# Attention and MLP in one kernel: a latest end for TensorE's side work in each step, and the first VectorE units one step sooner

## The chip, the core and the metric

The kernel runs on one core of a Trainium2 chip. The core has a matrix engine (TensorE, PE in the profile; its weight loads are listed as PEld), VectorE (DVE), ScalarE (ACT), GpSimd (POOL) and SyncE (SP), which here issues most of the DMAs. Each engine runs its own list of instructions in order, and the lists are tied together by semaphores. The metric is the device time of one execution in microseconds. It is given as the median of several runs.

## The reference

The kernel computes one block with an attention branch and an MLP branch on the same input, mixed by a gate for each token. Sizes: 2048 tokens, width 640, 32 heads of 20, MLP width 1536, bf16 inputs.

```python
def _A_ref(x, wqkv, wo):
    B, S, D = x.shape
    H = 32; Dh = D // H
    qkv = (x @ wqkv).reshape(B, S, 3, H, Dh).transpose(2, 0, 3, 1, 4)
    q, k, v = qkv[0], qkv[1], qkv[2]
    scores = jnp.einsum("bhqd,bhkd->bhqk", q, k) * Dh ** -0.5
    p = _softmax(scores, axis=-1)
    o = jnp.einsum("bhqk,bhkd->bhqd", p, v)
    return o.transpose(0, 2, 1, 3).reshape(B, S, D) @ wo

def _B_ref(x, w1, b1, w2):
    h = jnp.einsum("bsd,df->bsf", x, w1) + b1
    sp = jnp.log1p(jnp.exp(-jnp.abs(h))) + jnp.where(h > 0, h, 0)
    act = h * jnp.tanh(sp)
    return jnp.einsum("bsf,fd->bsd", act, w2)

g = _sigmoid((x * gate_w).sum(-1, keepdims=True))
return g * _A_ref(A_x, A_wqkv, A_wo) + (1 - g) * _B_ref(A_x, B_w1, B_b1, B_w2)
```

## The kernel before, in words

**Units and slots.** The attention is cut into units. A unit is one head (j, four heads to a group g), one tile of 128 keys (kt) and one chunk of 512 queries (c): a score matmul of 32 x 128 weights against 512 columns gives 128 x 512 scores in one PSUM bank. There are 32 heads x 16 tiles x 4 chunks = 2048 units. Three units make a slot, so there are 683 slots (the last has two units). The score banks are two sets of three banks. Slot s uses set s mod 2, so the scores of slot s can only be written once the exponential of slot s - 2 has read its set.

**The exponential of a slot.** ScalarE takes the exponentials of a whole slot in one ACTIVATE (line 1083): 128 x 1536, a *wide* one. In some slots the third unit is given to VectorE instead. ScalarE then takes only two units, 128 x 1024, a *narrow* one. VectorE works its unit out in four operations: it moves the scores out of PSUM with scale and bias (line 1111), and then runs three polynomial steps (lines 1127 and 1129) that build the exponential in the bits of an integer. The function `choose` decides whether a slot gives a unit away, by the planner's estimate of how much VectorE has left to do. Results of ScalarE go to a ring of five buffers (ETS).

**Products with v.** When the four heads of a key tile have their exponentials, TensorE multiplies them with v in one pass (four matmuls side by side, line 1197, function `emit_pv`), and sums up in the PSUM bank ACC over the 16 key tiles of a group. The units of VectorE get passes of their own (`emit_off`).

**Fillers.** All other matmuls are tasks that are worked off in pieces between the score blocks: the projections for q, k and v (lines 541, 607, 629, 705, 732), the Gram matrices for a safety bound (774), the MLP's two layers (851 and 910) and the output projection (934). Some are *forced*: when their due step has come they are issued at once, whatever the time. TensorE also gets passes without use (`spin`, line 1471, and repeated score blocks) where the planner finds it too thinly used.

**The planner.** The order is written by Python code before the program is built. A class `Plan` keeps an estimated time for each engine (`pl.now`) and adds every instruction's cost, with waits, as it is put in an engine's list. A loop goes over the steps. In step s it puts in: forced tasks that are due, the exponential of slot s, the choice for slot s + 2 and its score block, then up to two passes of products with v (`emit_pv(step, 2)`), then fillers as long as they end before `limit`, and then VectorE's work that fits. So on TensorE, what is put in after the score block of slot s + 2 in step s stands ahead of the score block of slot s + 3.

Costs that matter here, in us, as the planner has them: a wide exponential 1.335 (`EXP`), a narrow one 0.908 (`EXP_PAIR`), a pass of 512 columns 0.213 (`PASS`), a change of the kind of matmul 0.1 (`SWITCH`), a hop between engines 0.1 (`HOP`). Before the change the fillers' limit is the estimated end of the exponential of the step plus one wide exponential and a hop, whatever comes next; the products with v have no limit. `CALM` is the step from which `choose` is asked: slot `CALM` + 2 is the first that may give a unit away.

A second plan (`full`) stands in the program for inputs whose scores are too large for the fast exponential; a flag worked out on the chip chooses it, and with these inputs it does not run. Each engine loads that flag once (line 1399).

Of the kernel before, what the change touches and what calls it, by code (L numbers as in the profile page):

```python
# [47 lines left out]
SWITCH = 0.1  # L48
COL = 1 / 2400.0
PASS = CW * COL  # L50
EXP = 1.335
STREAM = 0.48
SPUN = 0.6
EXP_PAIR = 0.908
# [24 lines left out]
LAG = 9  # L79
SPARE = 3.5  # L80
WINDOW = 3.41
CALM = 4
PACKED = 10
PACKED_Q = 12
Q_AT = 100
# [3 lines left out]
H_AT = 150  # L89
H_STEP = 12.5  # L90
THIN = 0.09
OVER = 0.2
CUTS = ((0, 256), (256, 256))

# [124 lines left out]
def bass_gated_mix__softmax_full_mha__dense_activation_mish__prompt_kernel(  # L219
# [114 lines left out]
    NSLOT = -(-NC * NG * NKT * HG // SLOT)  # L334


    off = {}
    off_units = {}

    def attention(pl, fast):  # L340
# [84 lines left out]
        def flush(done):  # L425

            while not done():
                ready = [lane for lane in soon if lane]
                first = min(ready, key=lambda lane: (lane[0][2]().t1 if lane[0][2] else 0.0, lane[0][3]))
                first.popleft()[1]()  # L430
# [595 lines left out]
        started = {}  # L1026
        queue = deque()
        hold = {"until": 0}
        acc_free = [m_acc if fast else pl.add("dve", lambda e: e.memset(PS[:, ACC, :], 1.0))]

        def compose(s, extra=None):
# [19 lines left out]
        def score_mms(s, some, deps):  # L1051

            op = None
            for r in range(max(len(subs(*u[:3])) for u in some)):
                began = False
                for i, (c, g, kt, j) in enumerate(some):
                    if r >= len(subs(c, g, kt)):
                        continue
                    tile, cols, of_q = subs(c, g, kt)[r]
                    cost = max(extent(c, g)[1] * COL, THIN)  # L1060
                    op = pl.add("pe", lambda e, i=i, g=real(g), tile=tile, j=j, cols=cols, c=c, of_q=of_q: e.matmul(  # L1061
# [99 lines left out]
        def emit_off(group, last, force=False):  # L1161

            mine = off_units.get(group, []) if fast else []
            begun = started.get((group, "off"), 0)
            there = 0
            while there < len(mine) and mine[there] in unit_done and (
                    force or unit_done[mine[there]].t1 + HOP <= pl.now["pe"]):
                there += 1
            whole = there == len(mine)
            if there - begun > 1 or last and whole:  # L1170
                rows = []
                for u in mine[begun:there]:
                    if not rows or u[3] in [v[3] for v in rows[-1]]:
                        rows.append([])
                    rows[-1].append(u)
                for row in rows:
                    lasts = pv([(u, ei(off_home[u]).bitcast(BF16)[:, 0::2], [unit_done[u]]) for u in row])
                    for k, u in enumerate(row):
                        ei_free[off_home[u]] = lasts[k]
                started[(group, "off")] = there  # L1180
            return whole
# [21 lines left out]
        def emit_pv(step, passes):  # L1203

            while passes and step >= hold["until"]:
                if not queue:
                    return
                c, g, kt, _ = queue[0][2]
                emit_off((c, g), False)
                n = HG - sum(u[2] == kt for u in off_units.get((c, g), ()) if fast)  # L1210
                if len(queue) < n:
                    return
                if kt == tiles(c, g) - 1 and not emit_off((c, g), True):
                    if step < NSLOT - 1:
                        return
                    flush(lambda: emit_off((c, g), True, True))
                passes -= 1
                some = [queue.popleft() for _ in range(n)]
                lasts = pv([(u, ETS[:, s % NETS, i, :], [e_op[s]]) for s, i, u in some])
                for k, (s, i, u) in enumerate(some):  # L1220
                    op = pv_slot[s] = lasts[k]
                    pv_left[s] -= 1
                if kt == tiles(c, g) - 1:
                    hold["until"] = step + PV_HOLD
                    group_done(c, g, step, op)
# [264 lines left out]
        for step in range(NSLOT + 40):  # L1490
            now["step"] = step
            if step >= NSLOT and not queue and not tasks and not any(k >= step for k in at):
                break

            for t in [t for t in tasks if t.forced and t.due <= step]:
                while now["open"] not in (None, t):
                    put(now["open"])
                while t in tasks:
                    put(t)
            if step < NSLOT:  # L1500
                emit_e(step)
            if fast and area[0] and not w2_load and len(h_done) >= FIRST and all(ei_free[(0, b)] != "busy" for b in range(3)):
                load_w2()
            if acts and safe(acts[0][0]) < pl.now["act"] and mish_free():
                acts.popleft()[1]()
            ahead = able = 0.0
            rate = behind = 0.0
            lag = max((step - t.due for t in tasks if not t.forced and t.ready() is None), default=0)
            for t in tasks:
                slack = max(1, t.due - AHEAD * t.forced - step)  # L1510
                ahead += t.left()
                rate = max(rate, ahead / slack)
                if t.forced or t is now["open"] or t.ready() is not None:
                    able += t.left()
                    behind = max(behind, able / slack)
            now["rate"] = rate
            if step + 2 < NSLOT:
                compose(step + 2, choose(step + 2) if fast and step >= CALM and (step < slot_of(0, 1, 0) or behind < CATCH_UP and (lag < LAG or backlog() < SPARE) and room()) else None)
                emit_s(step + 2)
                to_come = pv_ready() * PASS  # L1520
                if owed + rate > 0.1 and pick(pl.now["pe"] + 0.8):
                    to_come += min(owed + rate, 0.4)
                fill_up(to_come, False)

                if fast and step + 2 in off:
                    emit_x(step + 2)
            limit = pl.now["act"] + EXP + HOP if step < NSLOT else 1e9
            owed = min(owed + rate, 1.0) if step < NSLOT else 1e9
            if fast and step < NSLOT and now["open"] and now["open"].left() <= min(owed + OVER, limit - pl.now["pe"] - PASS - SWITCH):
                t = now["open"]  # L1530
                while t in tasks:
                    put(t)
                    owed -= t.cost
            emit_pv(step, 2 if step < NSLOT - 1 else 99)

            while owed > 0:
                t = pick(limit)
                if t is None:
                    break
                put(t)  # L1540
                owed -= t.cost
            fill_up(0.0, True)
            for fn in at.pop(step, []):
                fn()
            work(pl.now["act"] + 0.5 if step < NSLOT else 1e9)
# [112 lines left out]
    fast = Plan("f_")  # L1658
# [55 lines left out]
```

## Time and profile before

| | |
|---|---|
| time, median of 3 runs | 866.54 us (866.3 to 866.74) |
| profiled execution: its own time | 866.43 us |
| profiled execution: span from the first to the last instruction | 864.6 us |
| granted TensorE clock, mean | 0.999 |
| busy: ScalarE, VectorE, TensorE | 847.8, 829.4, 756.3 us |

In the rows of the profile, times are microseconds unless marked ns. A row of a group reads: line, engine, operation, tile written <- tiles read, shapes, count | busy time, mean ns of one | idle time of the engine just before them, and what ended most of it. A row of the timeline reads: start, length, engine, line, operation, count, and in brackets the engine's idle time before it with what ended it; neighbouring instructions of the same line and tile are merged into one row, which bears the shapes of the first. The lengths of merged rows run from the first start to the last end. In the row of the granted clock each digit is a fortieth of the span, and 9 is 90% or more. A row of the chain of waits reads: start, length, what, count.

### The profile page before, as it was taken

The page shows a single profiled execution, that of the slowest core. Times are in us where ns is not written, and L with a number is a line of the kernel's source. Part 1 is how long each engine was busy: PE and PEld are TensorE (multiplying, and loading weights), DVE is VectorE, ACT ScalarE, POOL GpSimd, SP SyncE. Part 2 cuts the span into 40 slices and gives each one's busy share as a digit, 9 for nine tenths or more (in the row PEclk, how much of TensorE's full clock was granted, in tenths as well). Part 3 has the DMA queues.
Part 4 walks back from the last instruction along what each step waited for, and adds up shares of the span by engine and source line. Part 5 has one row for each costly group of instructions (what it writes and reads, how often), then busy time and mean ns, then how long its engine had stood idle before and what let it go on. Part 6 is the DMA issues. An engine that isn't in the chain of part 4 may idle for free.

```text
span 864.6 us, 15494 instructions
## 1 busy us (share of the span) xinstructions
PE 756.3 (87%) x6342; PEld 259.5 (30%) x6342; DVE 829.4 (96%) x1330; ACT 847.8 (98%) x714; POOL 7.3 (1%) x14
## 2 busy tenths in 40 slices
PE   8988998889889888898888888898888888899886
PEld 3333332223322332232223333333322333333232
DVE  4799999999999999999999999999999999999996
ACT  6999999999999999999999999999999999999996
POOL 2000000000000000000000000000000000000000
PEclk9999999999999999999999999999999999999999
DMA  9711310012233221401111211112112211000001
GB/s 215 95 61 36 107 46 19 16 60 69 78 93 89 67 62 53 123 26 38 44 39 44 71 34 58 44 36 60 55 44 60 59 51 41 28 25 29 18 14 35
DMA packets 76318, 48.42 MB, mean 56 GB/s; under 512 B 22104, under 2 KB 71888, under 8 KB 76192
## 3 DMA queue, kind: packets, MB, share of 16 engines
q1 hardware_dynamic: 73872, 46.86, 20.1%
q8 instruction: 52, 0.85, 0.4%
q10 hardware_dynamic: 2256, 0.47, 0.3%
q0 software_dynamic: 112, 0.01, 0.1%
q14 instruction: 26, 0.21, 0.1%
HBM read 37.64 MB, written 7.52 MB: 52 GB/s over the span
## 4 chain that ended last, share of the span: by engine, by line
ACT 94%; PE 4%; DMA 1%; DVE 0%; issue 0%; SPq 0%
ACT ETS L1083 92%; ACT REG L884 2%; PE PS L1061 1%; PE PS L1197 1%; ACT W2R L884 1%; DMA OTN<-in_A_x_dram 1%; PE PS L607 0%; PE PS L910 0%; PE PS L670 0%; DVE HB L940 0%; PE PS L774 0%; PE PS L679 0%; PE PS L851 0%; PE PS L541 0%; PE PS L1471 0%
## 5 line engine op out<-in xcount | busy, mean ns | idle before, releaser
L1083 ACT ACTIVATE ETS<-PS 128x1536 bf16<-128x1536 f32 (+1 forms) x683 | 827.6, 1449 | 1.9 <-PE PS L1061 1.7
L1061 PE MATMUL PS<-QT,KT 32*128 32x512 bf16 (+1 forms) x2202 | 275.8, 377 | 95.3 <-ACT ETS L1083 82.7
L1197 PE MATMUL PS<-ETS,V_all 128*21 128x512 bf16 (+1 forms) x1875 | 212.3, 379 | 0.7 <-DVE OUNG L1275 0.4
L1061 PEld LDWEIGHTS PS<-QT,KT 32*128 32x128 bf16 x2202 | 68.4, 91 | 308.9 <-ACT ETS L1083 280.8
L1127 DVE SCALAR_TENSOR_TENSOR ER<-ER 128x512 f32<-128x512 f32 x114 | 77.9, 683 | 0.1
L1127 DVE SCALAR_TENSOR_TENSOR EM<-EM 128x512 f32<-128x512 f32 x114 | 77.7, 682 | 0.0
L1197 PEld LDWEIGHTS PS<-ETS,V_all 128*21 128x21 bf16 x1875 | 48.4, 89 | 92.9 <-issue 84.6
L910 PE MATMUL PS<-W2R,HB 128*128 128x320 bf16 x384 | 74.4, 302 | 0.4
L1111 DVE TENSOR_SCALAR REG<-PS 128x512 f32<-128x512 f32 x85 | 58.2, 685 | 1.9 <-PE PS L1061 1.0
L851 PE MATMUL PS<-XB,REG 128*128 128x256 bf16 x360 | 57.5, 275 | 1.5 <-DVE HB L861 0.9
L1111 DVE TENSOR_SCALAR XE<-PS 128x512 f32<-128x512 f32 x78 | 53.3, 686 | 5.3 <-PE PS L1061 4.3
L910 PEld LDWEIGHTS PS<-W2R,HB 128*128 128x128 bf16 x384 | 28.1, 97 | 38.6 <-issue 27.4
L851 PEld LDWEIGHTS PS<-XB,REG 128*128 128x128 bf16 x360 | 27.9, 97 | 29.1 <-issue 27.2
L861 DVE TENSOR_TENSOR HB<-PS,B1T 128x512 bf16<-128x512 f32 x48 | 32.8, 684 | 1.1 <-PE PS L851 0.9
L1471 PE MATMUL PS<-KT 128*128 128x512 bf16 x103 | 32.0, 385 | 0.0
L1127 DVE SCALAR_TENSOR_TENSOR EM<-REG 128x512 f32<-128x512 uint16 x43 | 29.4, 684 | 0.3
L1129 DVE SCALAR_TENSOR_TENSOR REG<-EM,REG 128x512 int32<-128x512 f32 x43 | 29.3, 681 | 0.0
L1127 DVE SCALAR_TENSOR_TENSOR ER<-REG 128x512 f32<-128x512 uint16 x42 | 28.7, 684 | 0.2
L1129 DVE SCALAR_TENSOR_TENSOR REG<-ER,REG 128x512 int32<-128x512 f32 x42 | 28.6, 681 | 0.0
L1127 DVE SCALAR_TENSOR_TENSOR EM<-XE 128x512 f32<-128x512 uint16 x39 | 26.8, 686 | 0.3
L1127 DVE SCALAR_TENSOR_TENSOR ER<-XE 128x512 f32<-128x512 uint16 x39 | 26.7, 686 | 0.3
L1129 DVE SCALAR_TENSOR_TENSOR XE<-EM,XE 128x512 int32<-128x512 f32 x39 | 26.6, 683 | 0.1
(136 smaller groups left out, 813.1 us busy)
## 6 DMA issues: line engine op xcount, KB each, us to landing
REG<-in_B_w_dram SPq DMA_DIRECT2D x36, 320.0 KB, 3.1
BCT<-SUMS SPq DMA_DIRECT2D x31, 256.0 KB
W2R<-in_B_w_dram SPq DMA_DIRECT2D x12, 320.0 KB, 3.2
KT<-KS SPq DMA_DIRECT2D x28, 128.0 KB
QT<-QS SPq DMA_DIRECT2D x112, 20.0 KB
QS<-WOQ SPq DMA_DIRECT2D x16, 128.0 KB, 1.7
KS<-OTN SPq DMA_DIRECT2D x16, 128.0 KB, 1.7
W2R<-in_B_w_dram SPq DMA_DIRECT2D x1, 1920.0 KB, 9.2
```

The lines of the kernel that those rows point to most:

```text
L851: return lambda e, bank: e.matmul(PS[:, bank, i * HW:(i + 1) * HW], w1b(n1)[:, f, i * P:(i + 1) * P], xt(c)[:, f, cols], start=(f == 0), s ...
L861: ev = dve(lambda e: e.tensor_tensor(hb, PS[:, bank, :].rearrange("p (i t) -> p i t", i=2), bias, ALU.add), [last, b_load, *guarded, *b_re ...
L884: ex = pl.add("act", lambda e: e.activation(U, h, AF.Tanh, scale=0.5, bias=-MISH_AT / 2), [ev, u_free[0]], cost=0.95)
L910: return lambda e, bank: e.matmul(PS[:, bank, 0:HALF], HB[:, hc % 2, f, t * P:(t + 1) * P], W2[:, f, half * HALF:(half + 1) * HALF], start ...
L1061: op = pl.add("pe", lambda e, i=i, g=real(g), tile=tile, j=j, cols=cols, c=c, of_q=of_q: e.matmul(scores(s)[:, i, cols], KT[32 * j:32 * j ...
L1083: e_op[s] = pl.add("act", lambda e: e.activation(ETS[:, s % NETS, 0:n, :], scores(s)[:, 0:n, :], AF.Exp, scale=SCALE, bias=LIFT if fast el ...
L1111: ev_op[s] = dve(lambda e: e.tensor_scalar(y, scores(s)[:, 2, :], SCALE * ULPS, BIAS, ALU.mult, ALU.add), [s_op[s], ei_free[b], *(wkv_read ...
L1127: piece(WIDE, lambda e, v=m if i else f, i=i: e.scalar_tensor_tensor(m, v, STEPS[i], v, ALU.add, ALU.mult), lambda i=i: () if i else [lane ...
L1129: piece(WIDE, lambda e: e.scalar_tensor_tensor(x, m, LAST_STEP, y, ALU.mult, ALU.add))
L1197: lasts[n] = pl.add("pe", lambda e, tile=tile, h=real(g) * HG + j, j=j, src=src[:, cols], of_q=of_q, count=count: e.matmul(PS[32 * j:32 * ...
L1471: pl.add("pe", lambda e: e.matmul(PS[:, bank, :], k[:, 0:P], k, start=True, stop=True), [free], cost=PASS, kind="S")
```

## The change

Three things are changed. A new variable `latest` holds, in each step of the fast plan, the estimated end of the exponential of the step plus the real widths (wide or narrow) of the next two exponentials, less a constant `REFILL` of 0.58 us. The fillers' limit becomes the smaller of the old limit and `latest`. In `emit_pv` a pass of products with v is put off to a later step when its end, with a switch, would be after `latest`; the last steps, which ask for 99 passes, are excepted. And `CALM` goes from 4 to 3, so slot 5 is the first that may give a unit to VectorE, not slot 6.

```diff
-CALM = 4
+CALM = 3
...
 THIN = 0.09
+REFILL = 0.58
 OVER = 0.2
...
         hold = {"until": 0}
+        latest = [1e9]
...
                     flush(lambda: emit_off((c, g), True, True))
+                if passes < 50 and pl.now["pe"] + PASS + (SWITCH if pl.kind != "V" else 0) > latest[0]:
+                    return
                 passes -= 1
                 some = [queue.popleft() for _ in range(n)]
...
             limit = pl.now["act"] + EXP + HOP if step < NSLOT else 1e9
+            latest[0] = 1e9
+            if fast and step + 2 < NSLOT:
+                latest[0] = pl.now["act"] + sum(EXP_PAIR if s in off else EXP for s in (step + 1, step + 2)) - REFILL
+                limit = min(limit, latest[0])
             owed = min(owed + rate, 1.0) if step < NSLOT else 1e9
```

Since the planner's estimates carry on from step to step, the whole order after the first slots is written anew. Counted in the fast plan's program: wide exponentials 457 after and 454 before, narrow ones 226 and 229, score matmuls of 512 columns 2075 and 2062, passes without use 102 and 103; the tasks are the same.

## The prediction

> **What bounds the kernel now.** I read the page first: busy times, granted clock, the chain that ended last, the costliest groups.
>
> ```profile
> span 864.6 us, 15494 instructions
> PE 756.3 (87%) x6342; PEld 259.5 (30%) x6342; DVE 829.4 (96%) x1330; ACT 847.8 (98%) x714; POOL 7.3 (1%) x14
> PEclk9999999999999999999999999999999999999999
> L1083 ACT ACTIVATE ETS<-PS 128x1536 bf16<-128x1536 f32 (+1 forms) x683 | 827.6, 1449 | 1.9 <-PE PS L1061 1.7
> ```
>
> ScalarE (ACT) is busy for 98% of the span with 683 exponentials, and the page charges only 1.9 us of idle time to them. A change that makes TensorE deliver scores earlier can win only what ScalarE loses by late scores, so that loss has to be measured first. Next, the groups with shapes kept apart.
>
> ```profile
> L1083 ACT ACTIVATE ETS<-PS 128x1536 bf16<-128x1536 f32 x454 | 649.3, 1585 | 1.2 <-PE PS L1061 1.0
> L1061 PE MATMUL PS<-QT,KT 32*128 32x512 bf16 x2062 | 267.5, 384 | 92.1 <-ACT ETS L1083 79.7 <-ACT KT L654 0.5 <-DVE KT L550 0.5
> L1083 ACT ACTIVATE ETS<-PS 128x1024 bf16<-128x1024 f32 x229 | 252.5, 1181 | 0.7 <-PE PS L1061 0.7
> ```
>
> There are 454 wide exponentials (three units) and 229 narrow ones (two units; all but the last leave a unit to VectorE). Score matmuls idle 79.7 us waiting for ScalarE and at no place long for VectorE's exponential units, so VectorE, though 96% busy, does not hold the scores back.
>
> Then ScalarE's timeline, asked for stretches of several lengths.
>
> ```profile
> 10.33 1.45 ACT L1083 ACTIVATE ETS<-PS 128x1536 bf16<-128x1536 f32 x1 [0.49 <-PE PS L1061]
> 10.33 8.17 ACT L1083 ACTIVATE ETS<-PS 128x1536 bf16<-128x1536 f32 x6 [0.49 <-PE PS L1061]
> 10.33 10.92 ACT L1083 ACTIVATE ETS<-PS 128x1536 bf16<-128x1536 f32 x9 [0.49 <-PE PS L1061]
> 21.58 34.09 ACT L1083 ACTIVATE ETS<-PS 128x1024 bf16<-128x1024 f32 x28 [0.33 <-PE PS L1061]
> 55.83 51.96 ACT L1083 ACTIVATE ETS<-PS 128x1024 bf16<-128x1024 f32 x44 [0.16 <-PE PS L1061]
> 108.07 100.80 ACT L1083 ACTIVATE ETS<-PS 128x1536 bf16<-128x1536 f32 x85 [0.29 <-PE PS L1061]
> 209.07 5.05 ACT L1083 ACTIVATE ETS<-PS 128x1536 bf16<-128x1536 f32 x4 [0.20 <-PE PS L1061]
> 369.06 44.66 ACT L1083 ACTIVATE ETS<-PS 128x1024 bf16<-128x1024 f32 x38 [0.19 <-PE PS L1061]
> 750.74 105.25 ACT L1083 ACTIVATE ETS<-PS 128x1024 bf16<-128x1024 f32 x88
> ```
>
> One wide exponential ends after 1.45 us, six (all wide) after 8.17: one more wide costs 6.72 / 5 = 1.344 us. The next three are narrow: (10.92 - 8.17) / 3 = 0.917. A unit moved from ScalarE to VectorE is worth 0.427 us. The chain of waits gives a longer quiet stretch and the price of a tanh of the MLP between exponentials:
>
> ```profile
> 108.07 58.26 ACT ETS L1083 x49
> 214.12 0.94 ACT W2R L884
> ```
>
> By the program's order those 49 are 31 wide and 18 narrow; 1.45 + 30 x 1.344 + 18 x 0.917 = 58.3. The pace holds without any loss.
>
> Now the whole stream. It starts at 10.33, its first exponential ends at 11.78, the last at 750.74 + 105.25 = 855.99: 844.2 us. At the pace above it needs 453 x 1.344 + 229 x 0.917 + 24 tanh x 0.94 = 608.8 + 210.0 + 22.6 = 841.4, with the unrounded pace (1.3437) 841.2. **ScalarE loses about 3.0 us to late scores in the whole stream.** Before it (10.3) and after it (8.6 us) lie ends that the change hardly touches.
>
> Where it loses them:
>
> ```profile
> 102.89 4.89 ACT L1083 ACTIVATE ETS<-PS 128x1536 bf16<-128x1536 f32 x4
> 106.00 0.39 PE L1061 MATMUL PS<-QT,KT 32*128 32x512 bf16 x3
> 106.33 0.82 PE L607 MATMUL PS<-XB,REG 128*128 128x512 bf16 x3
> 107.09 0.61 PE L1197 MATMUL PS<-ETS,V_all 128*21 128x512 bf16 x4
> 107.63 0.60 PE L1061 MATMUL PS<-QT,KT 32*128 32x512 bf16 x6
> 108.07 1.45 ACT L1083 ACTIVATE ETS<-PS 128x1536 bf16<-128x1536 f32 x1 [0.29 <-PE PS L1061]
> ```
>
> Between two blocks of scores (106.00 and 107.63) stand three filler passes and two products with v, 1.63 us in all. The four exponentials before are wide, wide, narrow, narrow: the score block of 107.63 had to be there after two narrow ones, 1.83 us. ScalarE's previous end is 107.78, its next 109.52: 1.74 instead of 1.344, 0.40 us lost. In the program's order all five restarts in the list above come after two narrow exponentials in a row. That is the pattern that the change aims at.
>
> **The change, part by part.** *The latest end.* In step s the products with v and the fillers may run until two real widths after the exponential of s, less 0.58 us. After wide + wide or wide + narrow that is 2.09 or 1.66 us, beyond the old filler limit of 1.435, so fillers change only before two narrow ones (1.816 - 0.58 = 1.24 us); the products get a limit for the first time. I counted the planned work between consecutive score blocks in both programs' order, priced by the planner's passes (a pass 0.213, a switch 0.1; the 1.63 us above come out as 1.59). Both have 77 places behind two narrow exponentials. Before, 38 hold more than 0.88 us of inserted work, 25 of them over 0.97; after, 3 and 2. Every loss of this trace that I could place lies at places with 0.73 or more, those above 0.15 us at 0.94 or more. So most of the 3.0 us should go. Three things stay:
>
> (a) The keys' projection task near the start is forced, so the limit passes it by. Rows of before:
>
> ```profile
> 18.55 0.39 PE L1061 MATMUL PS<-QT,KT 32*128 32x512 bf16 x3 [0.72 <-ACT ETS L1083]
> 19.74 0.39 PE L1061 MATMUL PS<-QT,KT 32*128 32x512 bf16 x3
> 20.39 0.82 PE L541 MATMUL PS<-XB,REG 128*128 128x512 bf16 x3
> 21.14 0.39 PE L1061 MATMUL PS<-QT,KT 32*128 32x512 bf16 x3
> ```
>
> Here the block after 19.74 comes 1.40 us later with one product and three passes. The changed program puts one pass of the five before and four behind that block: 1.40 + 0.21 = 1.61. The first narrow exponential is now the sixth, not the seventh: four narrow ones precede the late block and its exponential is wide; before, three preceded it and it was the fourth. Worked through: blocks at about 18.12, 19.10, 20.71, exponential 0.44 behind the last (21.58 - 21.14) at 21.15 where 20.64 was due. It loses 0.46, as before. (b) Where three narrow ones follow each other with 0.78 us inserted each time, the delay adds up to at most 0.1 at some four places: 0.25. (c) The single load of the safety flag on TensorE now stands behind two narrow exponentials.
>
> ```profile
> L1399 PEldq TENSOR_LOAD <-FLAG x1: 485/485/485, 208.0 to 208.0; - x1
> ```
>
> It takes 0.49 us, mostly beside the product and the filler ahead of it: 0 to 0.5, I take 0.15. Left over in all: 0.46 + 0.25 + 0.15 = 0.86.
>
> *Held products.* A product runs later, so its exponentials' buffer is freed later. The ring holds five. In the program's order the last product of an exponential stands 0 to 3 steps behind it before and after (2 steps: 48 times before, 64 after; 3: 2 and 1); only from 4 on would ScalarE wait. Cost 0, down to 0 gain.
>
> *Fewer units on VectorE.* The planner, with other times in its books, moves 226 exponentials' third units instead of 229. Three more wide ones: 3 x 0.427 = **+1.28 us** on ScalarE, the engine that sets the end. VectorE loses 3 x 4 operations of 0.68 us, off the path. Nothing covers the 1.28.
>
> ```profile
> L1127 DVE SCALAR_TENSOR_TENSOR ER<-ER 128x512 f32<-128x512 f32 x114 | 77.9, 683 | 0.1
> ```
>
> *First units one slot sooner.* It moves one narrow exponential forward; it is in the count. *Warm-keeping passes* (102 instead of 103) and repeated score blocks (33 instead of 31) fill TensorE's waits: 0.
>
> **Sum**, against the profiled execution (866.43, 0.11 under the median of 866.54): 866.43 - 3.0 + 0.86 + 1.28 = 865.57. I say **865.6 us**, 0.1% less. Bounds of the residue: 0 gives 864.7, 2.3 us (three quarters of today's loss) gives 867.0.
>
> **Rivals.** *The late scores only move (0.14).* Forced tasks and the products of VectorE's units are not under the limit, and what is held back has to run later in fuller steps. For it: the work behind two wide exponentials grows, though little (240 us of it in the program before, 245 after; steps with more than 1.2 us 16 and 16). Against it: behind wide ones the slack is 0.43 larger. The loss stays at 3.0, the three wide ones are paid: 867.7.
>
> *The clock falls (0.06; slower).* TensorE held back idles more in those stretches, and a slower clock would make every block late. Rows of the ten passes at the very start and of the same pass later:
>
> ```profile
> L496 PE MATMUL PS<-ETS 128*128 128x512 bf16 x10 | 4.4, 632 | 1.2 <-DVE ETS L483 1.2
> L1471 PE MATMUL PS<-KT 128*128 128x512 bf16 x103 | 32.0, 385 | 0.0
> ```
>
> At 632 instead of 385 ns TensorE's 756.3 / 683 = 1.11 us per slot become 1.82, against 844.2 / 683 = 1.24 that ScalarE allows: 0.58 us late per slot. It decides from the point where more than two slots in all run so; one stretch of three slots costs 1.7 (867.3), two such stretches 3.5, which is 869.1. Against: the granted clock is 9 in every slice, and the planner adds passes of its own where TensorE gets thin. [...] No row of before shows a fall.
>
> *Late starts all count (0.05; much faster).* Exponentials start closer together than they end.
>
> ```profile
> 97.09 10.69 ACT L1083 ACTIVATE ETS<-PS 128x1536 bf16<-128x1536 f32 x9
> ```
>
> From 97.09 to 102.89 (the row above) five exponentials start, three wide and two narrow: 5.80 us, where their ends take 5.865, so each start comes 12 ns closer. The mean wide one is recorded 1585 ns long, the first 1.45 us: starts run ahead, and a late start is partly repaid from that lead. If instead the lead were a pace that ScalarE could keep, starts 12 ns closer each time, 683 x 0.012 = 8.2 us more could be won: 857.4. Against: ends never come closer than 1.344, in 49 exponentials without a stop either.
>
> **Chances.** Forecast 0.72, the rivals 0.14, 0.06 and 0.05, anything else 0.03. A measurement of this kernel can tell about 0.2% (1.73 us) from no change, and that bound lies at 864.81 and 868.27. The forecast reaches below 864.81 only with next to no residue (0.05 of its 0.72). Faster: 0.05 + 0.05 = 0.10. Slower: the clock's 0.06, 0.02 of the first rival, 0.02 else = 0.10. The rest, 0.80, is within. Range: from 864.6 (no residue) to 867.8 (the loss only moves), which leaves out the two outer rivals and half of the rest.
>
> **What would show it.** Right: 457 wide and 226 narrow exponentials; the stream from 10.33 ends at about 855.1; restarts of ScalarE at about 21 and at the flag's load (near 215) remain, those near 108, 168, 209 and 369 are gone; the granted clock stays 9. Wrong: restarts at new places worth more than 1.7 us together; score matmuls that wait for VectorE; a stream shorter than 843.3 less 2, which would say that starts set the pace; a tail longer than 8.6 us.

## The result and the profile after

| | before | after |
|---|---|---|
| time, median | 866.73 us (866.3 to 867.14, 5 runs) | 870.77 us (870.27 to 873.54, 5 runs) |
| profiled execution: its own time, span | 866.43, 864.6 us | 870.27, 868.4 us |
| mean granted clock of TensorE | 0.999 | 0.993 |

The ratio is 1.0054, with a 95% interval of 1.0043 to 1.0065. The change makes the kernel 0.5% slower. The forecast was 0.1% faster (865.6 us, range up to 867.8). Executions of the changed programs below scatter by several us with their mean clock (with the multiplication later, from 865.78 us at 0.998 to 871.70 us at 0.988), so a median is given with its lowest run.

The page of after, in the same order as that of before:

```profile
span 868.4 us, 15510 instructions
PE 759.6 (87%) x6352; PEld 260.0 (30%) x6352; DVE 824.4 (95%) x1318; ACT 848.4 (98%) x714; POOL 7.3 (1%) x14
PEclk9999989999999999999999999999999999999999
L1085 ACT ACTIVATE ETS<-PS 128x1536 bf16<-128x1536 f32 (+1 forms) x683 | 830.0, 1524 | 5.2 <-PE PS L1063 5.0
```

The busy shares are nearly those of before. Two small marks differ: one 8 in the row of the clock, the sixth of 40 slices (109 to 130 us), and 5.2 us of idle time ahead of the exponentials instead of 1.9. The groups with shapes kept apart have the counts of the forecast, 457 and 226:

```profile
L1085 ACT ACTIVATE ETS<-PS 128x1536 bf16<-128x1536 f32 x457 | 664.0, 1661 | 2.7 <-PE PS L1063 2.6
L1085 ACT ACTIVATE ETS<-PS 128x1024 bf16<-128x1024 f32 x226 | 256.7, 1246 | 2.5 <-PE PS L1063 2.4
```

Where ScalarE restarts, by its timeline (start, length, and in brackets the idle time):

```profile
10.04 10.49 ACT L1085 ACTIVATE ETS<-PS 128x1536 bf16<-128x1536 f32 x9 [0.49 <-PE PS L1063]
20.86 90.02 ACT L1085 ACTIVATE ETS<-PS 128x1536 bf16<-128x1536 f32 x75 [0.33 <-PE PS L1063]
112.48 1.02 ACT L1085 ACTIVATE ETS<-PS 128x1024 bf16<-128x1024 f32 x1 [1.59 <-PE PS L1063]
113.95 1.45 ACT L1085 ACTIVATE ETS<-PS 128x1536 bf16<-128x1536 f32 x1 [0.44 <-PE PS L1063]
116.18 1.02 ACT L1085 ACTIVATE ETS<-PS 128x1024 bf16<-128x1024 f32 x1 [0.78 <-PE PS L1063]
117.80 1.45 ACT L1085 ACTIVATE ETS<-PS 128x1536 bf16<-128x1536 f32 x1 [0.59 <-PE PS L1063]
119.58 104.69 ACT L1085 ACTIVATE ETS<-PS 128x1536 bf16<-128x1536 f32 x88 [0.34 <-PE PS L1063]
```

Before lost its time in many small pieces, at 108, 168, 209, 369 us and elsewhere. Those four are gone, and the one at about 21 us stays, as forecast. New are five restarts within about 7 us. Measured between the ends of successive exponentials against the pace of the prediction (1.344 and 0.917), after loses 5.85 us where before loses 3.07: 4.28 at 112 to 121 us, 0.89 at 757 to 762 us, and 0.68 everywhere else.

The account of the span, after less before: +2.78 for late scores, +1.28 for three exponentials that became wide, -0.29 because the first exponential starts at 10.04 instead of 10.33, +0.08 at the tail: +3.85, against 868.4 - 864.6 = 3.8.

Stretches around the two places, before and then after (columns: stretch and its length, busy time of PE, PEld, DVE, ACT, POOL, then the granted clock, DMA share, GB/s):

```profile
106.00:112.00 6.00, 5.28 (x50) 2.10 (x50) 5.88 (x11) 5.71 (x5) 0.00 (x0) 1.00 0.14 46
112.00:122.00 10.00, 9.22 (x77) 3.01 (x76) 9.89 (x18) 10.00 (x10) 0.00 (x0) 1.00 0.19 57
```

```profile
106.00:112.00 6.00, 3.58 (x32) 1.49 (x32) 2.63 (x5) 4.88 (x4) 0.00 (x0) 1.00 0.16 60
112.00:122.00 10.00, 9.88 (x67) 2.86 (x66) 8.43 (x15) 7.37 (x7) 0.00 (x0) 0.66 0.15 47
```

```profile
753.90:757.30 3.40, 2.36 (x18) 0.86 (x15) 3.40 (x5) 3.18 (x4) 0.00 (x0) 1.00 0.00 0
757.30:760.70 3.40, 3.40 (x20) 0.61 (x18) 2.39 (x4) 3.18 (x3) 0.00 (x0) 0.51 0.03 9
```

From 106 to 112 us VectorE works 2.63 us instead of 5.88, and TensorE 3.58 instead of 5.28. After that the clock is down: 0.66 over ten microseconds is half speed for 6.8 of them, and 0.51 at 757 us is half speed for all 3.4. So at 112 us the stand of VectorE comes first, and the clock follows. (At 757 us VectorE is busy all the time ahead of the fall; that place is looked at below.) The chain of waits of after tells what VectorE stood for (start, length, what):

```profile
90.03 0.55 SPq L599
...
91.19 4.71 DMA KS<-OTN
...
95.92 0.52 SPq L599
...
97.04 4.63 DMA KS<-OTN
...
102.84 6.78 DMA BCT<-SUMS
...
109.64 0.69 DVE OTN L1247
110.33 0.60 DVE OTN L617
```

L599 fetches transposed keys from the scratch tensor KS, the DMA `KS<-OTN` is a write of projected keys into it, and `BCT<-SUMS` broadcasts the softmax reciprocals of a finished group. SyncE issues all of them in its own order, and in after two fetches stand *ahead* of the write of 91.19. SyncE's timeline of before over the same work:

```profile
90.96 0.35 SPq L577 DMA_DIRECT2D KS<-OTN  x1
91.35 1.11 SPq L598 DMA_DIRECT2D KT<-KS  x2
92.51 0.55 SPq L1278 DMA_DIRECT2D RR<-OUNG  x1
93.22 1.07 SPq L598 DMA_DIRECT2D KT<-KS  x2
96.93 0.35 SPq L577 DMA_DIRECT2D KS<-OTN  x1
97.33 0.42 SPq L1283 DMA_DIRECT2D SUMS<-RR  x1
99.77 1.11 SPq L598 DMA_DIRECT2D KT<-KS  x2
100.92 0.52 SPq L1288 DMA_DIRECT2D BCT<-SUMS  x1
```

There the write goes first, and the fetches that need it go out at 93.22, 2.26 us after its issue. In after the write lands 4.71 us after its issue, behind the two fetches of 128 KB. The fetches that need it go out at 95.92 only, so they now stand right ahead of the second write. That one is issued nearly when it was (97.04, before 96.93), but takes 4.63 us to land; in before the fetches behind it go out 2.84 us after its issue. All that stands behind in SyncE's list comes later by it, and the broadcast goes out at 102.84 instead of 100.92. VectorE, before and then after:

```profile
107.19 0.69 DVE L616 CAST OTN<-PS 128x512 bf16<-128x512 f32 x1
108.00 0.69 DVE L1243 TENSOR_TENSOR OTN<-OUNG,BCT 128x512 bf16<-128x512 f32 x1
```

```profile
109.64 0.69 DVE L1247 TENSOR_TENSOR OTN<-OUNG,BCT 128x512 bf16<-128x512 f32 x1 [3.37 <-DMA BCT<-SUMS]
110.25 0.68 DVE L617 CAST OTN<-PS 128x512 bf16<-128x512 f32 x1
```

The multiplication by the broadcast now stands *ahead* of the cast that empties a projection's bank (L617; before, L616 came first). VectorE reaches it at 106.27 (109.64 - 3.37), 1.7 us sooner than it ran in before (108.00). The broadcast lands at about 109.6, 1.6 us after that time. So VectorE stands for 3.37 us with the cast queued behind. TensorE's next filler waits for that cast, and the score block stands behind the filler:

```profile
108.25 0.39 PE L1063 MATMUL PS<-QT,KT 32*128 32x512 bf16 x3
110.99 1.07 PE L733 MATMUL PS<-REG,XB 128*128 128x160 bf16 x13 [2.35 <-DVE OTN L617]
112.00 0.44 PE L1063 MATMUL PS<-QT,KT 32*128 32x512 bf16 x3
```

That is the first 1.7 us of ScalarE's loss. The other 2.6 us are the four restarts behind it; the clock is at half from 112.2 to 119.0 us.

### The profile page after: what moved, and what is told of

It is laid out like the page before. It is cut to its first block, busy times and chain, and to the rows that moved or that the text cites. A ratio compares the mean times of both kernels' runs of the same rounds, so it can differ in the third digit from the quotient of the medians.

```text
span 868.4 us, 15510 instructions
## 1 busy us (share of the span) xinstructions
PE 759.6 (87%) x6352; PEld 260.0 (30%) x6352; DVE 824.4 (95%) x1318; ACT 848.4 (98%) x714; POOL 7.3 (1%) x14
## 4 chain that ended last, share of the span: by engine, by line
ACT 91%; PE 4%; DMA 2%; DVE 2%; SPq 1%; issue 0%; ACTq 0%
ACT ETS L1085 88%; ACT REG L885 2%; DMA KS<-OTN 1%; PE PS L1063 1%; DMA BCT<-SUMS 1%; SPq L599 1%; ACT W2R L885 1%; PE PS L608 1%; PE PS L497 1%; DMA RR<-OUNG 0%; PE PS L1199 0%; DVE EM L1129 0%; DVE ER L1129 0%; PE PS L935 0%; DVE XE L1113 0%; DVE OTN L617 0%
## 5 line engine op out<-in xcount | busy, mean ns | idle before, releaser
L1199 PE MATMUL PS<-ETS,V_all 128*21 128x512 bf16 (+1 forms) x1879 | 209.2, 381 | 0.6 <-ACT ETS L1085 0.5
L1199 PEld LDWEIGHTS PS<-ETS,V_all 128*21 128x21 bf16 x1879 | 48.1, 89 | 93.9 <-issue 86.2
L1475 PE MATMUL PS<-KT 128*128 128x512 bf16 x102 | 30.7, 384 | 0.0
L733 PE MATMUL PS<-REG,XB 128*128 128x160 bf16 (+1 forms) x240 | 23.9, 235 | 2.9 <-DVE OTN L617 2.3
L1131 DVE SCALAR_TENSOR_TENSOR XE<-ER,XE 128x512 int32<-128x512 f32 x38 | 25.9, 682 | 0.3 <-issue 0.2
```

What stands on the lines that cost most here:

```text
L733: return lambda e, bank: e.matmul(PS[:, bank, i * n:(i + 1) * n], xt(t // 4)[:, f, t % 4 * P:(t % 4 + 1) * P], WV[:, f, g * HD:g * HD + n] ...
L1131: piece(WIDE, lambda e: e.scalar_tensor_tensor(x, m, LAST_STEP, y, ALU.mult, ALU.add))
L1199: lasts[n] = pl.add("pe", lambda e, tile=tile, h=real(g) * HG + j, j=j, src=src[:, cols], of_q=of_q, count=count: e.matmul(PS[32 * j:32 * ...
L1475: pl.add("pe", lambda e: e.matmul(PS[:, bank, :], k[:, 0:P], k, start=True, stop=True), [free], cost=PASS, kind="S")
```

## The experiments

All ratios are against the kernel before on the same chip, with 95% intervals. `shift(engine, which, by)` moves one instruction by so many places in an engine's finished list and leaves all else alone.

| kernel | median us | lowest | ratio |
|---|---|---|---|
| after, multiplication later on VectorE | 868.91 | 865.78 | 1.0018 [1.0001, 1.0036] |
| after, write ahead of the fetches | 867.38 | 865.98 | 1.0004 [0.9991, 1.0017] |
| after, broadcast ahead of the fetches | 867.66 | 866.58 | 1.0011 [0.9997, 1.0024] |
| before, multiplication sooner | 870.92 | 869.73 | 1.0043 [1.0032, 1.0054] |
| latest end alone | 872.14 | 869.29 | 1.0049 [1.0033, 1.0064] |
| sooner first units alone | 866.46 | 865.91 | 0.9995 [0.9985, 1.0004] |
| after, landing of 7.5 us in the books | 872.40 | 871.02 | 1.0062 [1.0045, 1.0080] |
| the same, more warm passes | 869.22 | 866.28 | 1.0025 [1.0011, 1.0038] |
| before, warm passes of 32 rows | 888.97 | 884.71 | 1.0245 [1.0213, 1.0278] |
| write first, books by rows, 0.38 / 0.50 | 867.28 | 864.92 | 1.0004 [0.9995, 1.0014] |
| write first, books by rows, 0.36 / 0.46 | 867.66 | 865.27 | 1.0007 [0.9996, 1.0018] |
| write first, books by rows, 0.38 / 0.64 | 865.72 | 865.11 | 0.9991 [0.9981, 1.0002] |

**Is it the late broadcast?** Theory A says so: SyncE's order makes the broadcast late, VectorE stands in front of it, TensorE runs dry, its clock halves. Three kernels take one link each out of the changed program, and a fourth puts the wait into the kernel before.

```diff
+    shift("dve", third multiplication by the broadcast, +5)
```

> The changed kernel with one VectorE instruction moved: the third group's multiplication by the broadcast reciprocals (it waited 3.4 us at 109.6 us in the changed kernel's trace) stands five places later in VectorE's list; all else is the same program. Theory A (the broadcast lands late, VectorE's list stands still, then TensorE's, then the clock halves): the restarts of ScalarE between 112.5 and 119.6, worth 4.3 us, go, the clock stays full there, the time is 866.5 (870.8 - 4.3); the second stretch at half clock near 757 may stay (0.9 us). Theory B (the latest end thins TensorE there and the clock falls of itself): the clock falls near 112 all the same and at most the 1.7 us of the first restart goes: 869 to 870.8.

```diff
+    shift("sp", the write KS<-OTN of 91.19, to a place ahead of the two fetches of 90.03)
```

> The changed kernel with SyncE's list put as in the kernel before at one place: the write of packed keys that was issued at 91.19 stands ahead of the two key fetches of 90.03 and 90.62, not behind them. Theory A, with the queue's order as its cause: the write lands in about 2.2 us instead of 4.7, the fetches and writes after it come about 2.5 us sooner, the broadcast is issued at about 101 and lands at about 107.5; VectorE waits 1 to 1.5 us instead of 3.4, ScalarE's loss there falls from 4.3 to at most 1: 867 to 868. Theory C (the transfers are slow there for another reason, such as load on the DMA engines): the broadcast still lands at about 109.6 and nothing changes: 870.8. Theory B: 870.8 as well.

```diff
+    shift("sp", the broadcast BCT<-SUMS of 102.84, -2)
```

> The changed kernel with the third group's broadcast of the reciprocals two places sooner in SyncE's list, ahead of the two key fetches that were issued at 101.7 and 102.3. Theory A: the broadcast is issued when the sums have landed (101.9) instead of 102.84, and no longer shares the rings with two fetches just ahead of it; it lands 2 us or more sooner, VectorE waits 0.5 to 1.5 us instead of 3.4, and the loss of 4.3 us shrinks to 0 to 1.5: 866.5 to 868. If the broadcast takes its 6.8 us whatever stands ahead of it: lands at 108.7, 869.5 to 870.5. Theory B: 870.8.

```diff
# on the kernel before
+    shift("dve", third multiplication by the broadcast, -4)
```

> The kernel before, with the same multiplication (at 108.0 us in its trace, where it did not wait) four places sooner in VectorE's list, so that VectorE comes to it at about 105.3. Theory A: VectorE's list stands until the broadcast lands (between 105.5 and 108), TensorE's filler behind it stands, and if TensorE idles for 1.5 us or more the clock halves for some microseconds: 1 to 5 us slower, 867.7 to 871.7, with none of the change's limits in the program. Theory B: without the latest end there is no fall of the clock; at most the wait itself of 1 to 2 us: 866.7 to 868.

With the write first, SyncE, VectorE and ScalarE read (the last row is one unbroken run of 55 exponentials across 112 us):

```profile
90.15 0.35 SPq L578 DMA_DIRECT2D KS<-OTN  x1
90.55 1.11 SPq L599 DMA_DIRECT2D KT<-KS  x2
```

```profile
107.69 0.69 DVE L1247 TENSOR_TENSOR OTN<-OUNG,BCT 128x512 bf16<-128x512 f32 x1 [1.29 <-DMA BCT<-SUMS]
```

```profile
47.81 65.46 ACT L1085 ACTIVATE ETS<-PS 128x1536 bf16<-128x1536 f32 x55 [0.37 <-PE PS L1063]
```

The stand shrinks from 3.37 to 1.29 us, and of the 4.28 us lost at this place 0.49 are left. With the multiplication later, or the broadcast ahead of the fetches, nothing at all is lost there. SyncE and VectorE with the broadcast first:

```profile
102.31 0.54 SPq L1292 DMA_DIRECT2D BCT<-SUMS  x1
107.26 0.69 DVE L1247 TENSOR_TENSOR OTN<-OUNG,BCT 128x512 bf16<-128x512 f32 x1 [0.60 <-DMA BCT<-SUMS]
```

It is issued only half a microsecond sooner than in after, but without two fetches just ahead of it the multiplication can start 4.95 us after the issue, not 6.8; what in the queue makes that difference is not shown. In the kernel before, with only the multiplication four places sooner, VectorE and ScalarE read:

```profile
108.52 0.69 DVE L1244 TENSOR_TENSOR OTN<-OUNG,BCT 128x512 bf16<-128x512 f32 x1 [3.02 <-DMA BCT<-SUMS]
```

```profile
112.08 4.14 ACT L1084 ACTIVATE ETS<-PS 128x1536 bf16<-128x1536 f32 x3 [4.21 <-PE PS L1062]
```

This kernel is at half clock from 109.3 us for 6.8 us and takes 870.92 us: the time of the changed kernel, with no limit on TensorE's work in it. Theory A holds, for the stand and for the fall behind it. The 1.5 us of idling that it names for this kernel were the author's guess, and no run shows such a bound: in after the clock fell behind idles of TensorE of 2.35 and of 1.04 us, and stayed full behind one of 1.18 us (at 739 us), as it did in before behind one of 1.07 us (at 589 us). But the three cures do not all come back below before: their profiled runs lose 1.75, 1.69 and 3.03 us in all (before 3.07), and yet their medians are 0.4 to 1.9 us above it at mean clocks of 0.9934, 0.9965 and 0.9945 (before, in 52 runs of these and the next four kernels' sessions: 0.9982). The first was expected at 866.5 us and missed that by 2.4. Something lowers the clock in some runs without a stand.

**Which part of the change did it?** The two parts alone:

```diff
# after
-CALM = 3
+CALM = 4
```

> The change without its second part: the latest end stays, VectorE's first units come where they came before (CALM 4). 225 narrow exponentials by the program's order, and SyncE's list again has the key fetches ahead of the write. Theory A (that order makes the third group's broadcast late, VectorE stands, TensorE idles and its clock halves): a stand of VectorE of 2 to 4 us near 112 us, a clock fall behind it, 870 to 871 us as the changed kernel. Rival (the sooner first units made the tight place): no stand near 112 us, no loss of ScalarE over 1 us there, about 867 us (four narrow exponentials fewer than before, 4 x 0.427 = 1.7 us, against 1.5 to 2 us of late scores that go).

```diff
# before
-CALM = 4
+CALM = 3
```

> The kernel before with VectorE's first units one slot sooner and nothing else (CALM 3). SyncE's list keeps the write ahead of the fetches, 230 narrow exponentials. Theory A: no stand of VectorE near 112 us, clock full throughout, ScalarE loses about 3 us as before, one narrow exponential more: 866.3 us, within 0.1% of before. Rival (the sooner first units made the tight place): 869 to 871 us with a fall of the clock near 112 us.

The latest end alone gives the whole damage. VectorE and ScalarE there:

```profile
111.00 0.69 DVE L1247 TENSOR_TENSOR OTN<-OUNG,BCT 128x512 bf16<-128x512 f32 x1 [4.08 <-DMA BCT<-SUMS]
```

```profile
114.86 1.02 ACT L1085 ACTIVATE ETS<-PS 128x1024 bf16<-128x1024 f32 x1 [3.33 <-PE PS L1063]
```

The sooner first units alone change nothing that can be told (0.9995). It is the latest end that shifts the planner's estimates, and with them the order of SyncE and VectorE.

**Would a truer landing time cure it, and is TensorE too thin?** The planner takes the broadcast to land 4.7 us after its issue; 6.78 were measured.

```diff
-... "nr2", cost=0.55, tail=4.7)]
+... "nr2", cost=0.55, tail=7.5)]
```

> The change with one number of the plan's books corrected: the broadcast of the reciprocals is taken to land 7.5 us after its issue instead of 4.7 (measured 6.8 in the changed kernel). VectorE's multiplication then comes later in its list by itself, 229 narrow exponentials as before the change. Theory A: no stand of VectorE near 112 us; with the clock full ScalarE loses 1 to 1.7 us where before loses 3.1, no wide exponential is paid: 864.5 to 865.5 us in the undisturbed runs. Rival (holding TensorE's work back thins it so that its clock falls by itself): more than a third of the runs with a mean clock of 0.996 or less, median 867 or more, although nothing stands near 112 us.

```diff
# on top of the longer landing
-STREAM = 0.48
-SPUN = 0.6
+STREAM = 0.56
+SPUN = 0.68
```

> The kernel with the corrected landing, and more of the passes that only keep TensorE busy (STREAM 0.48 to 0.56, SPUN 0.6 to 0.68: 141 instead of 121 warm passes, 74 repeated score blocks; 227 narrow exponentials). If thin TensorE work is why the clock falls in some runs of the changed programs: fewer runs at a mean clock of 0.996 or less than the kernel with the corrected landing alone, median within 1 us of its best run, 865.5 to 866.5 us. If the falls have another reason: as many such runs, and 0.9 us (two narrow exponentials fewer) plus the repeats' late blocks on top, 866 to 868 us.

The times hoped for failed in both, though the loss near 112 us is zero in both. In the first the rival's numbers came out: all four runs have a mean clock of 0.99 or less, and the median is 872.40 us. But it is no clean test of thin work. It loses 6.92 us elsewhere, and part of that is a new wait in the group of wide exponentials:

```profile
L1085 ACT ACTIVATE ETS<-PS 128x1536 bf16<-128x1536 f32 x454 | 666.6, 1671 | 6.1 <-PE PS L1063 3.6 <-PE PS L1199 2.5
```

ScalarE waits 2.5 us for products with v (L1199), that is for a free buffer in the ring of five. In this program's order nine slots have their last product 3 or 4 steps behind the exponential (two of them 4); in the changed kernel there is one such slot, at 3. The corrected number moves the whole plan again, to a worse place. Its mean clock is 0.9885, with four falls of 3.4 us in the profiled run. With more passes placed by *time* the mean clock is still only 0.9919, with 9 of 10 runs at 0.996 or less, and the median of 869.22 us lies above both forecasts. It has the ring's wait too (0.7 us), so it does not settle by itself whether thin work was the reason.

**What does the clock go by?** I compared all traces so far: in each phase of 3.41 us (the length of the fall of after at 757 us), the time under matmuls, once by time and once with each moment weighted by the rows of the array that a matmul uses then (a score matmul has 32 of 128 rows). The three matmuls of a score block run side by side on different rows (a block takes 0.39 us, as long as one matmul), but here the block counts as 32 rows. The phases that end in a fall lie between 0.02 and 0.29 by rows; by time they lie between 0.06 and 0.63, among many that nothing followed. The fall of after at 757 us is the clearest: TensorE idles 1.04 us there, and then repeats a score block twice, which fills the time, but with matmuls of 32 rows. So I changed the rows alone, in the kernel before:

```diff
-k = KT[:, 0, 0:CW]
+k = KT[0:32, 0, 0:CW]
 ... e.matmul(PS[:, bank, :], k[:, 0:P], k, start=True, stop=True
+            , tile_position=(0, 0))
```

> The kernel before, with its 103 warm-keeping passes done by 32 instead of 128 rows of TensorE's array: same number, same places, same columns, so the same time on TensorE. It tells apart what the clock goes by. Theory R (by rows in use): in the traces so far every fall follows a phase of 3.41 us in which the time under matmuls, each weighted by rows/128, is below about 0.28 of the phase; counted so, before has 0.12 such phases a run and this kernel would have about 12; the mean clock falls from 0.998 to 0.98 or less, median 872 us or more, falls spread over the whole span. Rival (by time alone, whatever the rows): no change, mean clock 0.998, 866.3 to 867.1 us.

Its page, and the group of these passes:

```profile
PEclk9999998599999999599759999999999999999689
L1471 PE MATMUL PS<-KT 32*128 32x512 bf16 x103 | 46.6, 542 | 0.0
```

TensorE stays as busy as before (88% of the span) and the passes stand where they stood. Yet the mean clock falls to 0.94 and the time rises by 2.45% to 888.97 us, far over the 872 us from which theory R counted: the profiled run is at half clock for 102 us before the tail, in five stretches of 10 to 31 us. They are not spread over the whole span, as theory R had said. They begin at 149, 351, 364, 433 and 825 us, where the passes stand in groups (146 to 168, 350 to 373, 429 to 459 and 821 to 842 us); 71 of the 103 passes themselves run at half clock. Counted by time, this kernel's phases are as in before (0.13 a run under 0.42, against 0.05). The rival is out: the passes of 32 rows did not hold the clock (0.94), those of 128 rows in the same places did (0.998). The rows of the repeated score block in after, and of a block at half clock behind it, for comparison:

```profile
755.71 1.47 PE L1063 MATMUL PS<-QT,KT 32*128 32x512 bf16 x9 [1.04 <-ACT ETS L1085]
757.84 0.61 PE L1063 MATMUL PS<-QT,KT 32*128 32x512 bf16 x3
```

Phases of 3.41 us in one run (their start times summed up, divided by 3.41), outside the falls themselves, against the mean clock of all timed runs:

| kernel | under 0.42 by time | under 0.28 by rows | mean clock |
|---|---|---|---|
| before | 0.05 | 0.12 | 0.9982 |
| sooner first units alone | 0.10 | 1.05 | 0.9964 |
| after, write ahead of the fetches | 0.33 | 1.31 | 0.9965 |
| after, broadcast ahead of the fetches | 0.20 | 1.70 | 0.9945 |
| latest end alone | 1.48 | 1.96 | 0.9933 |
| after | 1.26 | 2.26 | 0.9928 |
| after, landing of 7.5 us | 4.16 | 3.13 | 0.9885 |

A fall of one phase takes 0.002 off the mean (half of 3.41 us in a span of 868). By rows the order is nearly that of the clocks. By time it is less so, and three kernels with a lower clock stand close to before. The bound of 0.28 was picked on these traces, so only the later kernels are tests of it, and it is rough; so are the counts, which change by up to a quarter with how phases at the edge of a fall are taken. "After, multiplication later" (1.35, clock 0.9934) falls more often than its count says, the last kernel below (0.86, clock 0.9981) less. Two more that the table leaves out fit badly: "the same, more warm passes" has between 1.6 and 2.0 such phases at a clock of 0.9919, and the books by rows with 0.36 / 0.46 (below) about 3 at 0.9947. If the rows of matmuls that run side by side are added up, the phases ahead of the falls up to here lie between 0.05 and 0.36, and the kernels come out in nearly the same order. So the kernel with passes of 32 rows shows that the rows made a difference (0.94 against 0.998); no run shows how a block of three counts.

Where the phases lie may have a part too. In every record here full and half clock change on a grid of 3.41 us (in after at 112.2, 119.0, 757.3 and 760.7 us), and the grid lies differently against the work in each. The wait of 1.04 us with the two repeats behind it stands near 752 us in all three cures. In the profiled run of one (broadcast first) a fall follows at 753.0 us, in those of the other two none does. That fits a clock that differs from run to run, but no run separates it from other reasons.

**Does it help the change?** The plan's books for warm passes, counted by rows, with the write first:

```diff
-self.passes.append((at + cost, cost))
+self.passes.append((at + cost, cost * rows))      # rows = 0.25 for a score matmul, else 1
-STREAM = 0.48
-SPUN = 0.6
+STREAM = 0.38
+SPUN = 0.5
...
+spin_s(step + 2)                                  # one full-row pass ahead of a repeated score block
 repeat_s(step + 2)
```

> The change with the write ahead of the two key fetches, and with the plan's books for the warm-keeping counted by rows: a score matmul (32 rows) counts a quarter, STREAM 0.38 and SPUN 0.50, and a repeated score block has a full-row pass ahead of it. 117 warm passes (before 103), 27 repeats, 228 narrow exponentials. Theory R: at most 0.3 falls a run (the write put first alone had about 1), ScalarE loses 1 to 1.7 us where before loses 3.1, one wide exponential more (+0.43): median 865 to 866 us, 0.1 to 0.2% under before. Rival (falls come by time alone or by chance): as many runs at a mean clock of 0.996 or less as with the write put first (4 of 10), median 867 to 868 us.

The next has the same edit with `STREAM` 0.36 and `SPUN` 0.46:

> As the kernel with the books by rows, with STREAM 0.36 and SPUN 0.46: 92 warm passes, 16 repeats, 227 narrow exponentials. Theory R: fewer falls than with the write put first alone (1 a run), more than with 0.38 and 0.50; median 865.5 to 866.8 us. Rival: fewer warm passes than before (103), so more falls than with the write put first alone, median 868 us or more.

The profiled run of the first is the best seen here: 864.92 us, 0.72 us lost in late scores, clock full to the last 4 us. But four of its 10 runs are at a clock of 0.996 or less, as many as with the write put first alone, and the median is 867.28: here the rival's numbers came out. The weaker setting has 7 such runs of 10 and 867.66: with fewer warm passes more falls, which at 7 against 4 may be chance, and not as many us as the rival said. The last kernel adds only passes in TensorE's waits:

```diff
-SPUN = 0.5
+SPUN = 0.64
```

> The kernel with the write first and the books by rows, STREAM 0.38, with SPUN 0.64 instead of 0.50: 136 full-row warm passes instead of 117 in TensorE's waits, 27 repeats and 228 narrow exponentials as there. Theory R (the clock goes by rows in use): fewer runs at a mean clock of 0.996 or less than its 4 of 10, median 865.2 to 866.3 us, 0.1 to 0.2% under before. Rival (what is left of the falls doesn't go by thin phases): the same share of such runs, median 867 us; or the added passes push score blocks back: the best run above 865.5 us.

```profile
L1085 ACT ACTIVATE ETS<-PS 128x1536 bf16<-128x1536 f32 x455 | 658.3, 1631 | 1.1 <-PE PS L1063 1.1
L1085 ACT ACTIVATE ETS<-PS 128x1024 bf16<-128x1024 f32 x228 | 255.1, 1215 | 0.4 <-PE PS L1063 0.4
```

None of its 12 runs is at a clock of 0.996 or less (mean 0.9981; before 0.9984 in the same session). Its median is 865.72 us, 1.06 under before in the same session; the interval (0.9981 to 1.0002) just includes no change. Its profiled run loses 1.45 us to late scores. So theory R's numbers came out. But a pass of 128 rows adds time under matmuls as well as rows, so this kernel does not set the one against the other; the kernel with passes of 32 rows does. Nor does the count by rows tell the two settings apart: with the phases that start in a fall left out it is 0.72 for `SPUN` 0.50 and for 0.64.

## Why the prediction was wrong

*The pace and the count of widths.* Right. 457 wide and 226 narrow exponentials came out, and the price of 0.427 us each closes the account of the span above.

*The latest end on ScalarE's losses.* Right for the mechanism that it looked at. The losses at 108, 168, 209 and 369 us are gone. Of the residue of 0.86, the forced projection costs 0.44 at 20.9 us (forecast 0.46 at 21.15), the flag's load 0.02 instead of 0.15, and the triples of narrow exponentials next to nothing instead of 0.25. A new 0.21 at 47.6 us comes from VectorE standing for the gather of a group's sums, the same kind of wait as at 112 us. Outside the two bad stretches that makes 0.68.

*Held products.* The ring of five did not matter in the changed kernel, as said. It did in the kernel with the longer landing time, where two slots reach the step from which the prediction said that ScalarE would wait.

*The step that failed* is the pricing of the inserted work itself: "I counted the planned work between consecutive score blocks in both programs' order." It took every filler as ready when its turn comes. That was never looked at for the changed order of SyncE and VectorE, although both lists come out of the same estimates that the change shifts. Two fetches ahead of one write, and one multiplication ahead of one cast, cost 4.28 us: more than the whole 3.0 that was to be won. The prediction's reading that VectorE "does not hold the scores back" was right for the order of before, and was carried over to an order in which VectorE does, by way of a filler. No row of before showed it, but both orders could be read before any run. Of the prediction's own signs of being wrong, the first came out: restarts at new places worth more than 1.7 us together.

*The clock.* The forecast let the clock stay full. The rival had the size: two stretches at 3.5 us together, and the four restarts behind the stand and the place at 757 us cost 2.58 + 0.89 = 3.47. The 2.58 are 0.65 for each of four exponentials, near the rival's 0.58 per slot. In part that is luck: 0.32 of the 0.89 is lost at the same wait in two kernels whose clock stayed full there, and the first 1.7 us, the stand itself, were in no rival. The rival took its 632 ns from passes at 1 to 6 us, where the profile gives a clock of 1.00, so it is not shown that a lower clock made them slow; at half clock a score block took 0.61 us instead of 0.39. The rival's reason was wrong at 112 us: TensorE did not get thin because it was held back, but because it stood behind VectorE, and the fall came on top. At 757 us TensorE had waited for ScalarE alone. There, and in the runs that fall without a stand, work held back may be the reason; the runs do not tell it from the rewritten order of all work. One reason against the rival, "the planner adds passes of its own where TensorE gets thin", did not hold: at 757 us it had added two repeats of a score block, matmuls of 32 rows, and the clock was at half for 3.41 us behind them. Nor did the falls need a long stretch without matmuls: after fell behind 2.35 us and 1.04 us of it, and the kernel with passes of 32 rows fell with TensorE 88% busy over the span. The falls of after last 3.41 us and twice that, 6.83.

*First units one slot sooner.* Taken as part of the count. Alone it is 0.9995 [0.9985, 1.0004].

*Open.* Whether columns and matmuls side by side bear on the clock as rows did (0.94 against 0.998), and why the kernel with the multiplication later falls so often (8 of its 10 runs at 0.996 or less). Also, what the latest end is worth with a settled clock is only bounded: the last kernel is 0.1% under before with an interval up to no change, and it carries the other edits too.

## What to carry to other kernels

Where one planner writes the lists of all engines, an edit for one engine is an edit of all: compare every engine's order around each cross-engine chain, and SyncE's DMA queue first: here a write that landed 4.71 us after its issue stood ahead of a broadcast that went out at 102.84 instead of 100.92 us. An instruction that waits for a DMA should stand behind the work that others need, not ahead of it: here it stood for 3.37 us ahead of one cast. When passes are added to hold TensorE's clock, count their rows: here 103 passes of 128 rows came with a mean clock of 0.998, and of 32 rows with 0.94.

## What the hardware showed that was not expected

- TensorE's clock changed with the rows in use at the same time under matmuls (87 and 88% of the span): 103 passes of 128 rows against 32 rows in the same places gave a mean clock of 0.998 against 0.94, and 867.03 against 888.97 us.
- Half clock comes in stretches of 3.41 us or a multiple of that (3.41 and 6.83 in after, up to 30.7 in the kernel with passes of 32 rows); a score block of three matmuls takes 0.61 instead of 0.39 us in them.
- A write of 128 KB landed 4.71 us after its issue with two fetches of 128 KB ahead of it on the queue, and by 2.26 us without them. A broadcast behind two such fetches could be used 6.8 us after its issue, and 4.95 us after it when it was issued ahead of them.
